# Reordering the opening of a fused linear-attention and SwiGLU kernel: last v pair on two engines, q tiles 1 and 3 moved, one k load merged

## The chip, the cores and the metric

The kernel runs on one core of one Trainium2 chip. The metric is device time in microseconds (us) of one execution; lower is better. "Median" is over the executions of one kernel in one measurement. Every profiled execution that is compared here had a granted TensorE clock of 0.99 or more. "Span" is the length of the profiled execution inside its trace; it is shorter than the device time of the same execution (before: 324.5 and 326.26).

## The reference

Eight batches of eight heads, 576 tokens and 64 columns go through a linear attention with cosine weights. Its output, 4608 rows of 512, goes through a root-mean-square norm and a gated feed-forward part.

```python
def phi(x, c, s):
    r = np.maximum(x, 0.0)
    return np.concatenate([r * c, r * s], axis=-1)
q_p = phi(q, cos_w, sin_w)
k_p = phi(k, cos_w, sin_w)
kv = np.einsum('bhsf,bhsd->bhfd', k_p, v)
z = np.sum(k_p, axis=2)
num = np.einsum('bhsf,bhfd->bhsd', q_p, kv)
den = np.einsum('bhsf,bhf->bhs', q_p, z)[..., None] + 1e-06
x = num / den                                   # then (4608, 512)
xn = x / np.sqrt(np.mean(x * x, -1) + 1e-06) * rms_g
g = xn @ w_gate                                 # 512 -> 1536
out = (g * sigmoid(g) * (xn @ w_val)) @ w_out   # 1536 -> 512
```

## The kernel before

In the timelines each engine's instructions come in the order of the calls (TensorE's from 17.26 to 21.15 us of the kernel before are the calls of the second block below, one after the other), so the code is read here as the order on each engine. A call names its engine (A is ScalarE, V is VectorE, G is GpSimd) or is TensorE's (names with pe, mm or nd; fillers keep TensorE busy with products that nothing reads). The names in the traces: `qp` is weighted q, `qpT` its transpose, `kvzs` the copy of k times v with z, `xt` a tile of x, `scr` its squares, `rs` the inverse root, `xn` the normalised x, `xnT` its transpose, `hT` the hidden activations, `vvm` and `vvt` the large and the small part of v in bf16, and `rk`, `rv`, `rq` what the loads bring.

The opening, from the last pieces of v to the first normalised tile (cut):

```python
    kvz_mm(0, low_banks, LOW)
    kvz_copy(A, 0, 0, low_banks[0], LOW)
    kvz_copy(A, 0, 1, low_banks[1], LOW)
    v_cast(V, 0, 3, 4, 0, 5)               # the last v pair, both on VectorE
    v_cast(V, 0, 3, 4, 5, NJ)
    kvz_mm(0, high_banks, (2, 3))
    nd_half(0, 0, 0, psV[0])               # first numerators, half a tile
    nd_post_half(0, 0, 0, psV[0])
    x_gain(0, 0, 0)                        # x times the gain, ahead of the inverse root
    q_tr_evac(A, 0, 1, psO[0][:, :], (0, 4))
    kvz_mm(0, high_banks, (3, 4))
    ...
    filler(7, psV[1][:, :])
    q_tr_pe(0, 2, psO[0][:, :])
    x_scale(0, 0)                          # then times the inverse root
```

The feed-forward part starts while q tiles 2 and 3 of batch 0 are still to be transposed:

```python
    q_phi(A, 0, 3, 1)
    q_tr_evac(A, 0, 2, psO[0][:, :])
    x_norm(0, 1)
    q_phi(V, 0, 3, 0)
    open_ffn(0, (0, 1), 0, 128)            # steps 0 and 1, first 128 tokens
    x_tr_pe(0, 1, psV[1][:, :])
    x_tr_evac(V, 0, 1, psV[1][:, :])
    q_tr_pe(0, 3, psO[1][:, :])            # transposes of q tile 3 ...
    nd_pe(0, 2, psA)
    nd_post(0, 2, psA)
    q_tr_evac(A, 0, 3, psO[1][:, :])       # ... their copy ...
    x_sq(0, 2)
    wo_load(0)
    open_ffn(0, (0, 1), 128, 256)
    open_ffn(1, (2,), 0, 256, parts=(0,))
    nd_pe(0, 3, psA)                       # ... and the user of that copy
    nd_post(0, 3, psA)
```

The loads that matter later are all on SyncE's queue and are taken in order:

```python
    load_kv("k", 1, 0, 1)                  # one row of k of batch 1, in the prologue
    ...
    d = load_kv("k", 1, 1, 4)              # the other three rows, after most weights
    tc.add_manual_dep(d.ins, weight_dmas[5].ins.name, SYNC_DEP, reason="after most weights")
    gate_q = load_q(1)                     # q of batch 1, behind the gate weights
    ...
    w = wo_load(1)                         # output weights, behind q of batch 1
    tc.add_manual_dep(w.ins, gate_q.ins.name, SYNC_DEP, reason="after q of batch 1")
    ...
    at(0, 10, "post", q_phi, V, 1, 0, 0)   # weighted q of batch 1, behind step 10
    ...
    if (which, nb) == ("v", 3):            # pieces of v of batch 3, behind steps 13 and 14
        at(b, 13, "post", load_heads, "v", nb, 0, 4)
        at(b, 14, "post", load_heads, "v", nb, 4, 8)
        at(b, 14, "post", load_last, "v", nb)
```

Of the kernel before, what the change touches and what calls it, by code (L numbers as in the profile page):

```python
# [9 lines left out]
FP32 = mybir.dt.float32  # L10
BF16 = mybir.dt.bfloat16
AF = mybir.ActivationFunctionType
ALU = mybir.AluOpType
# [13 lines left out]
def kernel(  # L27
# [11 lines left out]
    nc = tc.nc  # L39
    B, H, S, D = q.shape  # L40
    DM = H * D
# [32 lines left out]
    def load_kv(which, b, r0=0, r1=4, j0=0, j1=NJ):  # L74

        key = (which, b)
        if key not in raw:
            raw[key] = (two if which == "k" else one).tile(
                [P, 4, NJ * D], FP32, name=f"r{which}", tag=f"r{which}"
            )  # L80
        src = {"k": k, "v": v}[which]
        return nc.sync.dma_start(
            out=raw[key][:, r0:r1, j0 * D : j1 * D],
            in_=src[b, 2 * r0 : 2 * r1, :, :]
            .rearrange("h s d -> (h s d)")
            .rearrange("(r p n) -> p r n", p=P, n=NJ * D)[:, :, j0 * D : j1 * D],
        )
# [80 lines left out]
    load_kv("v", 0, 3, 4, 0, 5)  # L168
    load_kv("v", 0, 3, 4, 5, NJ)
    load_q_tokens(4, NJ)  # L170
    load_kv("k", 1, 0, 1)
    nc.scalar.preload_act_table(AF.Silu)
    gb = one.tile([P, DM], FP32, name="gb")

# [106 lines left out]
            src = flat[:, 2048:2304].rearrange("p (i d) -> p i d", d=D)  # L281
        phi(eng, kp_of(b)[:, 8 * c : min(8 * c + 8, 36), o], src, f(c))

    def q_phi(eng, b, c, part):
        o = slice(0, D) if part == 0 else slice(D, F)
        f = cos_of if part == 0 else sin_of
        if (b, c) not in qp_tiles:
            qp_tiles[(b, c)] = four.tile(
                [P, H if c < 4 else 4, F], BF16, name="qp", tag="qp" if c < 4 else "qpt"
            )  # L290
        if b == 0:
            for i in range(2 if c < 4 else 1):
                j = 2 * c + i
                f = cos_of if part == 0 else sin_of
                phi(
                    eng, qp_tiles[(b, c)][:, 4 * i : 4 * i + 4, o],
                    raw[("q", 0)][:, :, j * D : (j + 1) * D], f(5 + j),
                )
            return
        src = view4(raw[("q", b)], c) if c < 4 else raw[("qt", b)][:, :, :]  # L300
        phi(eng, qp_tiles[(b, c)][:, :, o], src, f(c))
# [15 lines left out]
    def q_tr_pe(b, c, bank):  # L317
        t = qp_tiles[(b, c)]
        dst = bank.bitcast(BF16).rearrange("p (h s) -> p h s", s=P)
        for h in range(H if c < 4 else 4):  # L320
            nc.tensor.transpose(dst[:, h, :], t[:, h, :], ident[:, :])  # L321

    def q_tr_evac(eng, b, c, bank, heads=(0, 8)):
        h0, h1 = heads if c < 4 else (0, 4)
        if b == 0:
            src = bank.bitcast(BF16).rearrange("p (i h s) -> p h i s", i=2, h=H)
            copy(
                eng, q_dst(b, c)[:, h0:h1, :].rearrange("p h (i s) -> p h i s", i=2),
                src[:, h0:h1, :, :],
            )  # L330
            return
        dst = bank.bitcast(BF16).rearrange("p (h s) -> p h s", s=P)
        copy(eng, q_dst(b, c)[:, h0:h1, :], dst[:, h0:h1, :])
# [7 lines left out]
    def v_cast(eng, b, r0=0, r1=4, j0=0, j1=NJ):  # L341
        copy(
            eng, vvm[b % 2][:, r0:r1, j0:j1, 0:D],
            raw[("v", b)][:, r0:r1, j0 * D : j1 * D].rearrange("p r (j d) -> p r j d", d=D),
        )
# [34 lines left out]
    def kvz_mm(b, banks, rs=(0, 4)):  # L380

        for r in range(*rs):
            for j in range(NJ):
                for c in range(2):
                    lo = 64 * c
                    nc.tensor.matmul(  # L386
                        banks[c][:, r * E : (r + 1) * E],
                        lhsT=kp_main[b][lo : lo + 64, j, r, :],
                        rhs=vvm[b % 2][lo : lo + 64, r, j, :],
                        start=(j == 0), stop=(j == NJ - 1),  # L390
                    )
# [4 lines left out]
    def kvz_copy(eng, b, c, bank, rs=(0, 4)):  # L396
        if (b, c) not in kvzs:
            kvzs[(b, c)] = three.tile([P, 4 * E], BF16, name="kvzs", tag=f"kvzs{c}")
        lo, hi = rs[0] * E, rs[1] * E
        copy(eng, kvzs[(b, c)][:, lo:hi], bank[:, lo:hi])  # L400
# [75 lines left out]
    def x_sq(b, j):  # L476
        xt = x_of[(b, j)]
        scr = one.tile([P, DM + 1], BF16, name="scr", tag="scr")
        ms = four.tile([P, 1], FP32, name="ms", tag="ms")
        nc.scalar.activation(  # L480
            out=scr[:, :], in_=xt[:, 0 : DM + 1], func=AF.Square,
            scale=1.0 / math.sqrt(DM), accum_out=ms[:, :],
        )
        rs = four.tile([P, 1], FP32, name="rs", tag="rs")
        nc.gpsimd.tensor_tensor(out=rs[:, :], in0=ms[:, :], in1=mhalf[:, :], op=ALU.pow)  # L485
        rs_of[(b, j)] = rs

    xn_of = {}
    xg = three.tile([P, DM], FP32, name="sg", tag="sg")

    def x_gain(b, j, g):

        c = slice(g * DM // 2, (g + 1) * DM // 2)
        nc.vector.tensor_tensor(
            out=xg[:, c], in0=x_of[(b, j)][:, c], in1=gb[:, c], op=ALU.mult
        )

    def x_scale(b, j):
        xn = four.tile([P, DM], BF16, name="xn", tag="xn")
        nc.vector.tensor_scalar(  # L500
            out=xn[:, :], in0=xg[:, :], scalar1=rs_of[(b, j)][:, :], scalar2=None, op0=ALU.mult
        )
        xn_of[(b, j)] = xn

    def x_norm(b, j):
        xn = four.tile([P, DM], BF16, name="xn", tag="xn")
        nc.vector.scalar_tensor_tensor(  # L507
            out=xn[:, :], in0=x_of[(b, j)][:, 0:DM], scalar=rs_of[(b, j)][:, :], in1=gb[:, :],
            op0=ALU.mult, op1=ALU.mult,
        )  # L510
        xn_of[(b, j)] = xn
# [22 lines left out]
    def x_tr_evac(eng, b, j, bank, part=(0, 4)):  # L534
        dst = bank.bitcast(BF16).rearrange("p (t s) -> p t s", s=P)
        copy(eng, x_dst(b, j)[:, part[0] : part[1], :], dst[:, part[0] : part[1], :])
# [54 lines left out]
    def filler(n, bank):  # L591
        for _ in range(n):
            nc.tensor.matmul(bank, lhsT=warm[:, 0:P], rhs=warm[:, :], start=True, stop=True)  # L593
# [25 lines left out]
    def gval_slice(c0, c1):  # L619
        weight_dmas.append(weight_slice(wg, moe_w_gate, c0, c1))  # L620
        weight_dmas.append(weight_slice(wv, moe_w_val, c0, c1))
# [29 lines left out]
    low_banks = [psG[1][:, :], psV[1][:, :]]  # L651
    high_banks = [psA[:, c, :] for c in range(2)]
    kvz_mm(0, low_banks, LOW)
    kvz_copy(A, 0, 0, low_banks[0], LOW)
    kvz_copy(A, 0, 1, low_banks[1], LOW)
    v_cast(V, 0, 3, 4, 0, 5)
    v_cast(V, 0, 3, 4, 5, NJ)
    kvz_mm(0, high_banks, (2, 3))
    nd_half(0, 0, 0, psV[0])
    nd_post_half(0, 0, 0, psV[0])  # L660
    x_gain(0, 0, 0)
    q_tr_evac(A, 0, 1, psO[0][:, :], (0, 4))
    kvz_mm(0, high_banks, (3, 4))
    kvz_copy(A, 0, 0, high_banks[0], HIGH)
    kvz_copy(A, 0, 1, high_banks[1], HIGH)
    filler(1, idle)
    nd_half(0, 0, 1, psO[1])
    nd_post_half(0, 0, 1, psO[1])
    q_tr_evac(A, 0, 1, psO[0][:, :], (4, 8))
    q_phi(A, 0, 2, 1)  # L670
    x_sq(0, 0)
    nd_pe(0, 1, psA)
    nd_post(0, 1, psA)
    x_gain(0, 0, 1)
    q_phi(A, 0, 2, 0)
    x_sq(0, 1)
    gval_slice(768, 1152)
    gval_slice(1152, 1536)
    filler(7, psV[1][:, :])
    q_tr_pe(0, 2, psO[0][:, :])  # L680
    x_scale(0, 0)

    def open_ffn(pair, steps, c0, c1, first=0, parts=(0, 1)):

# [26 lines left out]
    for half, (eng, bank) in enumerate(((A, psG[1]), (V, psV[1]))):  # L711
        part = (2 * half, 2 * half + 2)
        x_tr_pe(0, 0, bank[:, :], part)
        x_tr_evac(eng, 0, 0, bank[:, :], part)
    q_phi(A, 0, 3, 1)
    q_tr_evac(A, 0, 2, psO[0][:, :])
    x_norm(0, 1)
    q_phi(V, 0, 3, 0)
    open_ffn(0, (0, 1), 0, 128)
    x_tr_pe(0, 1, psV[1][:, :])  # L720
    x_tr_evac(V, 0, 1, psV[1][:, :])
    q_tr_pe(0, 3, psO[1][:, :])
    nd_pe(0, 2, psA)
    nd_post(0, 2, psA)
    q_tr_evac(A, 0, 3, psO[1][:, :])
    x_sq(0, 2)
    wo_load(0)
    open_ffn(0, (0, 1), 128, 256)
    open_ffn(1, (2,), 0, 256, parts=(0,))
    nd_pe(0, 3, psA)  # L730
    nd_post(0, 3, psA)
    open_ffn(1, (3,), 0, 256, first=1, parts=(0,))
    x_norm(0, 2)
    open_ffn(1, (2, 3), 0, 256, parts=(1,))
    open_h(0, 0, 0)
# [34 lines left out]
    def at(blk, n, where, f, *args):  # L770
        slots.setdefault((blk, n), none())[where].append((f, args))
# [2 lines left out]
        for f, args in slots.get((blk, n), none())[where]:  # L774
            f(*args)

    d = load_kv("k", 1, 1, 4)
    tc.add_manual_dep(d.ins, weight_dmas[5].ins.name, SYNC_DEP, reason="after most weights")
    gate_q = load_q(1)
    tc.add_manual_dep(  # L780
# [10 lines left out]
    for j in range(NJ):  # L791
        at(0, 7 + max(0, j - 1) // 2, "post", k_phi, V, 1, j, 0)
        at(0, 7 + max(0, j - 1) // 2, "post", k_phi, A, 1, j, 1)
    at(0, 10, "post", q_phi, V, 1, 0, 0)
    at(0, 11, "post", q_phi, A, 1, 0, 1)


# [216 lines left out]
```

## Time and profile before

| | before |
|---|---|
| median of 3, then of 6 runs | 326.24 us, 326.26 us |
| span of the profiled execution | 324.5 us |
| TensorE busy | 316.2 us, 97% |
| first matmul of the feed-forward part | 17.26 us |
| first 512-column matmul, which ends the opening | 29.98 us |
| first transpose of q of batch 1 | 41.20 us |
| first product of k and v of batch 3 | 97.47 us |
| end of the last copy of an output tile | 321.19 us |

The last rows are marks on TensorE's timelines. Between two marks TensorE does the same products in every kernel of this study (the fillers lie ahead of the first mark), so a difference in the distance between two marks is waiting time. That is the tool of this document: effects of some tenths of a microsecond are lost in the time of a whole run but stand out in such a distance. TensorE's timeline of the kernel before, with start, length, engine, line, operation, output and inputs, shapes, count:

```profile
29.98 1.03 PE L546 MATMUL psG<-xnT,wg 128*128 128x512 bf16 x3
...
41.20 0.61 PE L321 MATMUL psV<-ident,qp 128*128 128x128 bf16 x8
...
97.47 0.29 PE L370 MATMUL psA<-vvm,kpm 128*128 128x65 bf16 x4
97.59 0.19 PE L370 MATMUL psA<-vvt,kpm 128*128 128x65 bf16 x1
```

There is no bracket with an idle time at any of the four: TensorE waits for nothing there. The last two lines show that the product on the small part of v follows 0.12 us behind that on the large part.

### The profile page before, as it was taken

How to read it: one execution, taken by the hardware profiler on the slowest of the kernel's cores; microseconds unless marked ns; L12 is line 12 of the kernel's file. 1: busy time of each engine (PE TensorE's matmuls, PEld its weight loads, DVE VectorE, ACT ScalarE, POOL GpSimd, SP SyncE). 2: the span in 40 equal slices, each digit the busy share in tenths (PEclk: the TensorE clock that was granted, in tenths of full speed). 3: DMA queues.
4: the chain of work that ended last, by engine and by line, in shares of the span. 5: the costliest groups of instructions: out<-in, count | busy, mean ns of one | idle time of the engine just before them, and what ended most of it. 6: DMA issues, size and time to landing. Idle time of an engine off the chain costs nothing.

```text
span 324.5 us, 6131 instructions
## 1 busy us (share of the span) xinstructions
PE 316.2 (97%) x2249; PEld 162.4 (50%) x2284; DVE 184.3 (57%) x398; ACT 173.8 (54%) x351; POOL 39.3 (12%) x85
## 2 busy tenths in 40 slices
PE   8999999999999999999999999999999999999995
PEld 3588465555445444554454445444544444444443
DVE  6875768787656765578267745772577133203410
ACT  6974865965665556645555466455644333223321
POOL 4660202001111110012001120120011000000000
PEclk9999999999999999999999999999999999999999
DMA  7999999898799775977597679856611400020014
GB/s 271 281 196 253 309 205 339 243 165 189 164 248 273 190 205 153 237 163 195 165 214 206 155 219 210 194 158 215 128 40 33 131 32 0 25 106 0 1 33 100
DMA packets 89377, 53.90 MB, mean 166 GB/s; under 512 B 56321, under 2 KB 81921, under 8 KB 89346
## 3 DMA queue, kind: packets, MB, share of 16 engines
q1 hardware_dynamic: 82304, 48.65, 57.4%
q0 software_dynamic: 6880, 4.72, 10.0%
q8 instruction: 18, 0.29, 0.4%
q10 hardware_dynamic: 162, 0.13, 0.2%
q14 instruction: 13, 0.11, 0.1%
HBM read 37.75 MB, written 9.44 MB: 145 GB/s over the span
## 4 chain that ended last, share of the span: by engine, by line
PE 93%; DVE 2%; ACT 2%; issue 1%; POOL 0%; DVEq 0%
PE psC L566 26%; PE psV L546 26%; PE psG L546 26%; PE psA L414 2%; PE psO L593 2%; PE psA L370 2%; PE psG L566 2%; PE psO L692 1%; PE psG L692 1%; PE psV L692 1%; PE psV L321 1%; ACT kpm L252 1%; PE psA L386 1%; ACT sg L555 0%; PE psA L422 0%
## 5 line engine op out<-in xcount | busy, mean ns | idle before, releaser
L561 DVE TENSOR_TENSOR hT<-psV,sg 128x512 bf16<-128x512 f32 x102 | 70.3, 689 | 96.0 <-PE psV L546 71.2
L555 ACT ACTIVATE sg<-psG 128x512 f32<-128x512 f32 x102 | 60.6, 594 | 64.5 <-PE psG L546 63.2
L546 PE MATMUL psV<-xnT,wv 128*128 128x512 bf16 (+1 forms) x365 | 92.1, 375 | 0.4
L546 PE MATMUL psG<-xnT,wg 128*128 128x512 bf16 (+1 forms) x352 | 90.9, 375 | 0.7
L566 PE MATMUL psC<-wo,hT 128*128 128x512 bf16 x382 | 88.2, 380 | 0.7
L546 PEld LDWEIGHTS <-wv 128*128 128x128 bf16 x416 | 40.6, 98 | 47.4
L566 PEld LDWEIGHTS <-hT 128*128 128x128 bf16 x420 | 40.2, 98 | 46.7
L546 PEld LDWEIGHTS <-wg 128*128 128x128 bf16 x416 | 38.5, 98 | 40.8 <-DVE xnT L339 0.4
L485 POOL TENSOR_TENSOR rs<-ms,mhalf 128x1 f32<-128x1 f32 x36 | 19.8, 549 | 187.6 <-ACT scr L480 187.6
L337 ACT COPY osb<-psC 128x512 f32<-128x512 f32 (+1 forms) x33 | 19.1, 579 | 43.1 <-PE psC L566 42.4
L507 DVE SCALAR_TENSOR_TENSOR xn<-xt,rs,gb 128x512 bf16<-128x512 f32 x35 | 26.5, 757 | 16.4 <-POOL rs L485 16.3
L480 ACT ACTIVATE scr<-xt 128x513 bf16<-128x513 f32 x36 | 22.9, 635 | 23.7 <-DVE xt L469 23.6
L252 ACT ACTIVATE kpm<-rk,tab 128x256 bf16<-128x256 f32 (+2 forms) x58 | 28.2, 545 | 1.5 <-DMA rk<-in_k_dram 1.5
L469 DVE TENSOR_TENSOR xt<-psA,rec 128x512 f32<-128x512 f32 x35 | 24.2, 691 | 1.2
L252 ACT ACTIVATE qp<-rq,tab 128x512 bf16<-128x512 f32 (+1 forms) x37 | 23.7, 661 | 0.0
L254 DVE TENSOR_SCALAR kpm<-rk,tab 128x128 bf16<-128x128 f32 (+2 forms) x64 | 20.5, 377 | 2.1 <-DMA rk<-in_k_dram 2.1
L254 DVE TENSOR_SCALAR qp<-rq,tab 128x512 bf16<-128x512 f32 (+1 forms) x37 | 16.0, 452 | 0.0
L414 PEld LDWEIGHTS <-qpT 128*128 128x128 bf16 x248 | 11.7, 98 | 6.7 <-issue 0.3
L414 PE MATMUL psA<-kvzs,qpT 128*128 128x65 bf16 x248 | 12.8, 194 | 0.3
L546 PE MATMUL psG<-xnt_tail,wg 128*128 128x512 bf16 x48 | 12.3, 379 | 0.1
L546 PE MATMUL psV<-xnt_tail,wv 128*128 128x512 bf16 x47 | 12.1, 379 | 0.0
L339 DVE CAST vvm<-rv 128x1024 bf16<-128x1024 f32 (+4 forms) x16 | 10.4, 674 | 0.0
(99 smaller groups left out, 183.8 us busy)
## 6 DMA issues: line engine op xcount, KB each, us to landing
out_dram<-osb SPq DMA_DIRECT2D x28, 256.0 KB, 2.5
rk<-in_k_dram SPq DMA_DIRECT2D x20, 256.0 KB, 3.2
rq<-in_q_dram SPq DMA_DIRECT2D x20, 256.0 KB, 3.1
rv<-in_v_dram SPq DMA_DIRECT2D x16, 256.0 KB, 3.2
rq<-in_q_dram SPq DMA_DIRECT2D x2, 1024.0 KB, 9.2
out_dram<-osb SPq DMA_DIRECT2D x14, 128.0 KB, 3.2
rv<-in_v_dram SPq DMA_DIRECT2D x3, 576.0 KB, 8.4
wo<-in_moe_w_out_dram POOLq DMA_DIRECT2D x4, 384.0 KB, 7.1
```

What stands on the lines that cost most here:

```text
L252: nc.scalar.activation(out=out_ap, in_=in_ap, func=AF.Relu, scale=scale)
L254: eng.tensor_scalar(out=out_ap, in0=in_ap, scalar1=scale, scalar2=0.0, op0=ALU.mult, op1=ALU.max)
L337: nc.scalar.copy(out=o, in_=i)
L414: nc.tensor.matmul(o[:, g, i, :], lhsT=qpT[(b, 0)][:, h, j * P : (j + 1) * P], rhs=kvz_of(b, h), start=True, stop=True,)
L469: nc.vector.tensor_tensor(out=xt[:, 0:DM].rearrange("p (b h d) -> p b h d", b=2, d=D), in0=o[:, :, :, 0:D], in1=rec[:, :, :].unsqueeze(3). ...
L480: nc.scalar.activation(out=scr[:, :], in_=xt[:, 0 : DM + 1], func=AF.Square, scale=1.0 / math.sqrt(DM), accum_out=ms[:, :],)
L485: nc.gpsimd.tensor_tensor(out=rs[:, :], in0=ms[:, :], in1=mhalf[:, :], op=ALU.pow)
L507: nc.vector.scalar_tensor_tensor(out=xn[:, :], in0=x_of[(b, j)][:, 0:DM], scalar=rs_of[(b, j)][:, :], in1=gb[:, :], op0=ALU.mult, op1=ALU. ...
L546: nc.tensor.matmul(pst[bank][:, cols[0] : cols[1]], lhsT=w[:, t, n * P : (n + 1) * P], rhs=x[:, t, cols[0] : cols[1]], start=(t == 0), sto ...
L555: nc.scalar.activation(out=sg[:, :], in_=psG[bank][:, :], func=AF.Silu)
L561: nc.vector.tensor_tensor(out=hTs[blk][:, n, :], in0=psV[bank][:, :], in1=sg[:, :], op=ALU.mult)
L566: nc.tensor.matmul(bank, lhsT=hTs[blk][:, n, j * P : (j + 1) * P], rhs=wo[:, n, :], start=(n == 0), stop=(n == NNT - 1),)
```

## The change

The intent is an earlier first x tile and fewer waits of TensorE in the opening. **Part 1**: the last v pair is cast by ScalarE and VectorE side by side, and all its products come ahead of the first numerators; the copies of q tile 1 stand behind them. **Part 2**: the gain and the inverse root are applied to x tile 0 in one combined multiply, as to all other tiles. **Part 3**: q tile 3 is transposed later, behind the work of two x tiles. **Part 4**: the first weighted q of batch 1 moves from behind step 10 to behind step 11 on VectorE. **Part 5**: the early load of one row of k of batch 1 is gone; the later load brings all four rows.

```diff
-    load_kv("k", 1, 0, 1)
...
+    v_cast(A, 0, 3, 4, 0, 5)
+    v_cast(V, 0, 3, 4, 5, NJ)
+    kvz_mm(0, high_banks, HIGH)
     kvz_copy(A, 0, 0, low_banks[0], LOW)
     kvz_copy(A, 0, 1, low_banks[1], LOW)
-    v_cast(V, 0, 3, 4, 0, 5)
-    v_cast(V, 0, 3, 4, 5, NJ)
-    kvz_mm(0, high_banks, (2, 3))
     nd_half(0, 0, 0, psV[0])
     nd_post_half(0, 0, 0, psV[0])
-    x_gain(0, 0, 0)
-    q_tr_evac(A, 0, 1, psO[0][:, :], (0, 4))
-    kvz_mm(0, high_banks, (3, 4))
...
+    x_norm(0, 0)
...
-    filler(7, psV[1][:, :])
-    q_tr_pe(0, 2, psO[0][:, :])
-    x_scale(0, 0)
+    filler(9, psV[1][:, :])
...
+    q_tr_pe(0, 2, psO[0][:, :])
+    q_tr_evac(A, 0, 2, psO[0][:, :])
     q_phi(A, 0, 3, 1)
-    q_tr_evac(A, 0, 2, psO[0][:, :])
     x_norm(0, 1)
-    q_phi(V, 0, 3, 0)
+    q_phi(V, 0, 3, 0, (0,))
     open_ffn(0, (0, 1), 0, 128)
     x_tr_pe(0, 1, psV[1][:, :])
     x_tr_evac(V, 0, 1, psV[1][:, :])
-    q_tr_pe(0, 3, psO[1][:, :])
+    q_phi(V, 0, 3, 0, (1,))
     nd_pe(0, 2, psA)
     nd_post(0, 2, psA)
+    open_ffn(0, (0, 1), 128, 256)
+    q_tr_pe(0, 3, psO[1][:, :])
     q_tr_evac(A, 0, 3, psO[1][:, :])
     x_sq(0, 2)
     wo_load(0)
-    open_ffn(0, (0, 1), 128, 256)
     open_ffn(1, (2,), 0, 256, parts=(0,))
+    open_ffn(1, (3,), 0, 256, first=1, parts=(0,))
     nd_pe(0, 3, psA)
     nd_post(0, 3, psA)
-    open_ffn(1, (3,), 0, 256, first=1, parts=(0,))
...
-    d = load_kv("k", 1, 1, 4)
+    d = load_kv("k", 1)
...
-    at(0, 10, "post", q_phi, V, 1, 0, 0)
+    at(0, 11, "post", q_phi, V, 1, 0, 0)
```

More of the change, by code (lines that the diff above doesn't have):

```diff
@@ L282, in k_phi_as_q, with q_phi @@
         phi(eng, kp_of(b)[:, 8 * c : min(8 * c + 8, 36), o], src, f(c))
-    def q_phi(eng, b, c, part):
+    def q_phi(eng, b, c, part, subs=(0, 1)):
         o = slice(0, D) if part == 0 else slice(D, F)
@@ L291, in q_phi @@
         if b == 0:
-            for i in range(2 if c < 4 else 1):
+            for i in subs if c < 4 else (0,):
                 j = 2 * c + i
@@ L488 @@
     xn_of = {}
-    xg = three.tile([P, DM], FP32, name="sg", tag="sg")
-    def x_gain(b, j, g):
-        c = slice(g * DM // 2, (g + 1) * DM // 2)
-        nc.vector.tensor_tensor(
-            out=xg[:, c], in0=x_of[(b, j)][:, c], in1=gb[:, c], op=ALU.mult
-        )
-    def x_scale(b, j):
-        xn = four.tile([P, DM], BF16, name="xn", tag="xn")
-        nc.vector.tensor_scalar(
-            out=xn[:, :], in0=xg[:, :], scalar1=rs_of[(b, j)][:, :], scalar2=None, op0=ALU.mult
-        )
-        xn_of[(b, j)] = xn
     def x_norm(b, j):
@@ L653 @@
     kvz_mm(0, low_banks, LOW)
+    v_cast(A, 0, 3, 4, 0, 5)
+    v_cast(V, 0, 3, 4, 5, NJ)
+    kvz_mm(0, high_banks, HIGH)
     kvz_copy(A, 0, 0, low_banks[0], LOW)
     kvz_copy(A, 0, 1, low_banks[1], LOW)
-    v_cast(V, 0, 3, 4, 0, 5)
-    v_cast(V, 0, 3, 4, 5, NJ)
-    kvz_mm(0, high_banks, (2, 3))
     nd_half(0, 0, 0, psV[0])
     nd_post_half(0, 0, 0, psV[0])
-    x_gain(0, 0, 0)
-    q_tr_evac(A, 0, 1, psO[0][:, :], (0, 4))
-    kvz_mm(0, high_banks, (3, 4))
     kvz_copy(A, 0, 0, high_banks[0], HIGH)
     kvz_copy(A, 0, 1, high_banks[1], HIGH)
-    filler(1, idle)
     nd_half(0, 0, 1, psO[1])
     nd_post_half(0, 0, 1, psO[1])
-    q_tr_evac(A, 0, 1, psO[0][:, :], (4, 8))
-    q_phi(A, 0, 2, 1)
+    q_tr_evac(A, 0, 1, psO[0][:, :])
     x_sq(0, 0)
@@ L673 @@
     nd_post(0, 1, psA)
-    x_gain(0, 0, 1)
-    q_phi(A, 0, 2, 0)
+    q_phi(A, 0, 2, 1, (0,))
+    q_phi(V, 0, 2, 0, (0,))
+    x_norm(0, 0)
+    q_phi(V, 0, 2, 0, (1,))
     x_sq(0, 1)
+    q_phi(A, 0, 2, 1, (1,))
     gval_slice(768, 1152)
     gval_slice(1152, 1536)
-    filler(7, psV[1][:, :])
-    q_tr_pe(0, 2, psO[0][:, :])
-    x_scale(0, 0)
+    filler(9, psV[1][:, :])
     def open_ffn(pair, steps, c0, c1, first=0, parts=(0, 1)):
```

## The prediction

> **What bounds the kernel now.** I read the busy table first, then the chain of waits, then the timelines of each engine from 8 to 31 us and from 39 to 46 us, where the diff acts.
>
> ```profile
> PE 316.2 (97%) x2249; PEld 162.4 (50%) x2284; DVE 184.3 (57%) x398; ACT 173.8 (54%) x351; POOL 39.3 (12%) x85
> ...
> PE 93%; DVE 2%; ACT 2%; issue 1%; POOL 0%; DVEq 0%
> ```
>
> TensorE is busy 97% and holds 93% of the chain that ends last. The diff removes no product that the result needs, so it can only move idle gaps of TensorE. Nearly all of those that it touches lie in the opening, where the chain leaves TensorE:
>
> ```profile
> 14.56 0.72 ACT scr L480 x2
> 15.28 0.29 ACT qp L252
> ...
> 16.77 0.56 POOL rs L485
> 17.33 0.02 issue
> 17.36 0.75 DVE xn L507
> 18.11 0.82 DVE qp L254 x2
> 18.93 0.14 issue
> 19.07 0.38 PE psO L321 x4
> 19.45 0.25 PE psA L414 x8
> ```
>
> Columns are start, length, engine, tile. Squares of x tiles (scr), their inverse root (rs) and normalised tiles (xn) decide when TensorE has work; before 17.26 us it runs fillers (seven, 13.87 to 15.55 us). From 17.26 us it works on the feed-forward part. There it stands still twice more, for about 0.12 us before the first half of the transposes of q tile 3 and 0.31 us before the second (they wait for the qp at 18.11): 0.43 us in all. From 19.07 to 30 us I find no gap worth naming. So the opening has little left to win: at most those 0.43 us plus what an earlier first x tile gives.
>
> **What the Trainium skill says.** (1) Perfetto Trace Analysis, Optimization Strategy: find the gaps on the engine in question within one regime and ask what unblocks them; and its section on the most-contended engine warns that matmul busy time says little of headroom. The trace agrees: 97% busy includes fillers, so I count gaps, not percent. (2) VectorE: DVE Perf Modes, the perf-mode tier table: a tensor_scalar on fp32 in SBUF runs 2x, a tensor_tensor 1x, and a PSUM operand lowers the tier. The trace agrees in kind: scaling the first x tile by one scalar took 0.49 us, the combined multiply that replaces it takes 0.75 us. (3) ScalarE: Activation LUTs, Rules for kernel authors: about 0.3 us per ACTIVATE plus 0.83 ns per element. The trace has 0.676 us for a cast of 576 columns and 1.14 us for 1152, so 0.81 ns each and 0.21 us fixed. (4) DMA: Bandwidth & Descriptors, Queues, rings and completion order: each DMA engine goes round-robin between queues by packets. The trace agrees: from 26 to 30 us both queues move data, about 0.22 MB per us on the SyncE queue and 0.08 on the software queue.
>
> **Part 1, the last v pair and its products.** Now VectorE casts both pieces, 0.68 us from 11.31 us. After, ScalarE casts 320 columns: estimated from the two casts above as 0.21 + 320 x 0.81 ns = 0.47 us, in 11.22 to 11.69. ScalarE has 0.27 us idle there, so the copies of the low kv are about as late as now (11.60 instead of 11.58). The 36 high products, now in two parts ending at 12.72, run in one go and end near 12.2. First numerators start 12.08 instead of 11.90 and VectorE begins on them 0.14 later, at 12.50. It then does two half tiles of 0.83 us without the 0.42 us gain multiply between them: x tile 0 is whole at 14.07 instead of 14.46, 0.39 earlier.
>
> **Part 2, the first x tile's chain.** Square and accumulator read 0.73 us after a 0.10 wait (14.17 to 14.90), inverse root 0.57 (14.98 to 15.55; the weight issues leave GpSimd free from 14.72), then the combined multiply of 0.75 instead of 0.49: done 16.32 against 16.46. Of 0.39 us, 0.26 is paid back for the dearer multiply. Transposes and two evacuations follow as now (0.75 from transpose to first matmul): 17.10 instead of 17.26. The transposes of q tile 2 (8, 0.45 us) now fit into that evacuation wait, so they cost nothing; nor did they before, beside fillers. Two more fillers lie in idle time. **Gain 0.16 us.**
>
> **Part 3, the moved transposes of q tile 3.** Order on TensorE is now: steps 0 and 1 for 128 columns (0.90, to 18.00), transposes of x tile 1 (end of result 18.40), numerators of tile 2 (0.22), then steps 0 and 1 for the next 128 columns, which need VectorE's copy of x tile 1 (0.41 us, 18.42 to 18.83). With only the numerators in between, TensorE idles from about 18.5 to 18.87: 0.38 us. That takes the place of the 0.43 us gone. Then 0.90 us, the q transposes 0.45, their result at 20.38. The lines of now:
>
> ```profile
> 19.49 1.01 ACT L337 COPY qpT<-psO 128x1024 bf16<-128x1024 bf16 x1 [0.58 <-PE psO L321]
> ...
> 20.91 0.40 PE L414 MATMUL psA<-kvzs,qpT 128*128 128x65 bf16 x8
> ...
> 21.80 0.69 DVE L469 TENSOR_TENSOR xt<-psA,rec 128x512 f32<-128x512 f32 x1
> ...
> 22.40 0.74 DVE L507 SCALAR_TENSOR_TENSOR xn<-xt,rs,gb 128x512 bf16<-128x512 f32 x1
> ...
> 23.34 0.39 PE L532 MATMUL psA<-ident,xn 128*128 128x128 bf16 x4
> ```
>
> The copy of q tile 3 is done at 20.50 and numerators 3 come 0.41 us later: no wait. After the change the copy runs 20.42 to 21.42, and only two steps (0.87 us) lie between the transposes and numerators 3: TensorE is ready at 21.09 and idles to 21.46, **0.37 us**. The delay carries on: VectorE makes x tile 3 (it ends 1.58 us after those numerators began, 23.04) before it normalises x tile 2 (0.75, to 23.69), so the transposes of x tile 2 wait to 23.72, another **0.28 us**, and those of x tile 3 lose about 0.06. The squares of x tile 2 queue behind the 1.0 us copy, but their root is there by 22.70 and doesn't bind.
>
> Sum: -0.16 - 0.43 + 0.38 + 0.37 + 0.28 + 0.06 = 0.50; following the clock instead, the step after x tile 3 begins at 25.98 where it began at 25.55: **+0.43 us**, which I take. After it TensorE has no gap up to 30 us to win it back.
>
> **Part 4, the q work of batch 1, moved by a step.**
>
> ```profile
> 40.28 0.47 DVE L254 TENSOR_SCALAR qp<-rq,tab 128x512 bf16<-128x512 f32 x1
> 40.67 0.68 DVE L561 TENSOR_TENSOR hT<-psV,sg 128x512 bf16<-128x512 f32 x1
> ```
>
> TensorE begins the transposes that need this qp at 41.20. Behind the hT product, which cannot start before the step's last matmul ends near 40.51, the qp runs 41.13 to 41.60. TensorE waits from 41.20 to about 41.63: **+0.43 us**, with all times before shifted alike. Nothing fills it, since engines run in program order.
>
> **Part 5, the loads.** One row of k for batch 1 (288 KB) leaves the early queue and joins the later load of that k. The early one overlaps the first weights for only half a microsecond (12.0 to 12.5), so weights land some 0.3 us earlier; those were in time already. The later load grows from 864 to 1152 KB. It waits as now for the sixth weight slice (SyncE waited 16.6 us for it); estimated at the 0.22 MB per us above, its 1.18 MB take 5.4 us from about 25.6 and land near 32, while ScalarE first uses them at 33.26 plus the shift. q of batch 1 slips by about 0.5 us, to 39.2, ahead of use after 40.2. No wait; **0 us**.
>
> **Sum.** 0.43 + 0.43 = +0.86 us: 326.24 + 0.86 = 327.10.
>
> **The rivals.** (a) The author's aim holds: the opening ends 0.2 to 0.4 us sooner, because TensorE never waits for the q copy or the x copy. For it: x tile 0 is ready 0.39 us earlier and the idle 0.12 and 0.31 disappear. Against it: the 1.01 us copy with 0.87 us of work before its user. It would give about 325.9. I give it 25%. (b) A load becomes the bound: the larger k load or the q behind it comes late, ScalarE stands before its k work, its Silu behind that, and TensorE waits. For it: the DMA engines are 90% busy throughout the opening, and the q work was moved back as if q came later. Against it: estimated margins of 1.4 us and more. It would add 0.5 to 1.5 us: about 328. I give it 15%. (c) My four waits come as worked out: 60%. (d) The late qp is hidden because TensorE waits there anyway: the trace shows none between 40.5 and 44 us, and it would take 0.43 off (c), inside the range.
>
> **Range and chances.** The weighted effect is 0.60 x 0.86 - 0.25 x 0.3 + 0.15 x 1.5 = +0.67, so 326.9. The range takes in (a) at its lower end and the milder cases of (b) at the upper: 325.9 to 327.6. Two per cent is 6.5 us; the whole opening holds under 2 us of TensorE gaps, so faster and slower by that much are near 1% each, slower a little likelier through loads.
>
> **What would show it.** In the timeline after: first matmul of the feed-forward part near 17.1; a gap near 18.5 to 18.9 before steps 0 and 1 of the second 128 columns; numerators 3 right behind a q copy ending near 21.4; transposes of x tile 2 near 23.7; the end of the opening (now 29.98, the first 512-column matmul) at 30.4; transposes of q of batch 1 right behind a VectorE qp, 0.86 us later than now, at 42.06. If the first 512-column matmul starts before 30.0, part 3 is wrong; if those q transposes come straight behind the output products, part 4 is; if ScalarE waits for a DMA at its k work of batch 1, part 5 is.

## The result and the profile after

The kernel got slower: a median of **328.30 us** (328.04 to 328.83, 6 runs) against 326.26 us (326.21 to 326.45, 6 runs). The ratio is 1.0064, with a 95% interval of 1.0051 to 1.0077. Here and below, a ratio is the mean time of one kernel's fast runs over that of the other's of the same rounds, so it is not quite the ratio of the medians. The prediction was 326.9 with a range up to 327.6, so the direction was right, but the loss of 2.04 us is outside the range and far above the 0.86 us of its own sum.

The page of the kernel after, busy time by engine and the chain by engine:

```profile
PE 318.2 (97%) x2285; PEld 162.1 (50%) x2285; DVE 184.2 (56%) x397; ACT 173.5 (53%) x349; POOL 39.7 (12%) x85
...
PE 87%; ACT 4%; DVE 3%; DMA 3%; SPq 1%; issue 1%; POOL 0%; ACTq 0%; DVEq 0%
```

TensorE's share of the chain fell from 93% to 87%, and DMA and SyncE's issue (SPq), which the chain before did not have, now hold 4%. Of this, 3.69 us is only the first load of k at the start, where the chain before ran over fillers; 7.79 us is a load of v at 91 to 99 us. So somewhere in the middle the end depends on a load. This is the first sign of what the prediction lacked. The opening in the chain of waits of the kernel after:

```profile
14.30 0.73 ACT scr L479 x2
...
15.11 0.67 POOL rs L484
...
15.80 0.76 DVE xn L490
...
18.67 0.43 DVE xnT L338
...
20.68 1.02 ACT qpT L336
...
21.75 0.43 PE psA L413 x8
...
22.64 0.69 DVE xt L468
...
24.05 0.40 PE psA L515 x4
```

The squares of x tile 0 begin 0.26 us earlier than before (14.30 against 14.56). Further down, the chain leaves TensorE at the three places that were foreseen: for the copy of x tile 1 (18.67), for the copy of q tile 3 (20.68, 1.02 long, with its user right behind it at 21.75) and for x tile 3 and what queues behind it (22.64), up to the transposes of x tile 2 at 24.05, which stood at 23.34 before.

The marks, in TensorE's timeline of the kernel after:

```profile
30.78 0.59 PE L529 MATMUL psG<-xnT,wg 128*128 128x512 bf16 x2
...
42.64 0.61 PE L320 MATMUL psV<-ident,qp 128*128 128x128 bf16 x8 [0.48 <-DVE qp L253]
...
98.91 0.28 PE L369 MATMUL psA<-vvm,kpm 128*128 128x65 bf16 x4
99.50 0.19 PE L369 MATMUL psA<-vvt,kpm 128*128 128x65 bf16 x1 [0.31 <-POOL vvt L338]
```

A bracket gives TensorE's idle time and what ended it. Two of the four marks have one now: the transposes of q of batch 1 wait for VectorE, and the first product on the small part of v of batch 3 waits for GpSimd's cast of it, 0.59 us behind the product before it where it was 0.12. The chain of waits says what the cast had waited for:

```profile
90.81 3.30 SPq L121
94.16 4.49 DMA rv<-in_v_dram
...
98.71 0.75 POOL vvt L338
```

That cast also took longer than before, and VectorE works on a cast of its own at that time. The kernel after, VectorE and GpSimd:

```profile
98.50 0.70 DVE L338 CAST vvm<-rv 128x1024 bf16<-128x1024 f32 x1
98.71 1.20 POOL L338 CAST vvt<-rv 64x256 bf16<-64x256 f32 x2 [6.87 <-DMA rv<-in_v_dram]
```

and before:

```profile
97.01 0.89 DVE L339 CAST vvm<-rv 128x1024 bf16<-128x1024 f32 x1
96.92 1.25 POOL L339 CAST vvt<-rv 64x256 bf16<-64x256 f32 x2 [6.52 <-DMA rv<-in_v_dram]
```

Before, GpSimd's first cast of the small v starts 0.09 us ahead of VectorE's cast of the large v, takes 0.43 us (to 97.35), and VectorE's takes 0.89. After, it starts 0.21 us behind VectorE's, takes 0.74 us (to 99.45) and ends 0.25 us after VectorE's has ended. So the later landing cost twice here: the cast started later and took longer.

The distances between the marks, worked out by subtraction from both traces, divide the whole difference (us):

| stretch | before | after | change | predicted |
|---|---|---|---|---|
| start to the first feed-forward matmul | 17.26 | 17.35 | +0.09 | -0.16 |
| from there to the first 512-column matmul | 12.72 | 13.43 | +0.71 | +0.59 |
| from there to q of batch 1 | 11.22 | 11.86 | +0.64 | +0.43 |
| from there to the first product of batch 3 | 56.27 | 56.27 | 0.00 | 0 |
| from there to the product on the small v | 0.12 | 0.59 | +0.47 | 0 |
| from there to the end of the last copy | 223.60 | 223.58 | -0.02 | 0 |
| from the last copy to the end of the span | 3.30 | 3.69 | +0.39 | 0 |
| span | 324.5 | 326.8 | +2.3 | +0.86 |

Two rows are what was predicted, somewhat larger. Two rows, 99 us and the tail, are nowhere in the prediction: 0.86 us together.

### The profile page after: what moved, and what is told of

It is laid out like the page before. It is cut to its first block, busy times and chain, and to the rows that moved or that the text cites. A ratio compares the mean times of both kernels' runs of the same rounds, so it can differ in the third digit from the quotient of the medians.

```text
span 326.8 us, 6161 instructions
## 1 busy us (share of the span) xinstructions
PE 318.2 (97%) x2285; PEld 162.1 (50%) x2285; DVE 184.2 (56%) x397; ACT 173.5 (53%) x349; POOL 39.7 (12%) x85
## 4 chain that ended last, share of the span: by engine, by line
PE 87%; ACT 4%; DVE 3%; DMA 3%; SPq 1%; issue 1%; POOL 0%; ACTq 0%; DVEq 0%
PE psC L549 25%; PE psG L529 25%; PE psV L529 25%; PE psA L413 2%; ACT kpm L251 2%; PE psA L369 2%; DMA rv<-in_v_dram 1%; PE psG L549 1%; DMA rk<-in_k_dram 1%; SPq L121 1%; PE psG L671 1%; PE psA L385 1%; PE psV L671 1%; PE psO L671 1%; PE psV L320 1%
## 5 line engine op out<-in xcount | busy, mean ns | idle before, releaser
L529 PE MATMUL psG<-xnT,wg 128*128 128x512 bf16 (+1 forms) x368 | 92.8, 374 | 0.1
L549 PE MATMUL psC<-wo,hT 128*128 128x512 bf16 x396 | 89.4, 379 | 0.0
L251 ACT ACTIVATE qp<-rq,tab 128x512 bf16<-128x512 f32 (+1 forms) x35 | 22.8, 669 | 0.0
L253 DVE TENSOR_SCALAR qp<-rq,tab 128x512 bf16<-128x512 f32 (+1 forms) x39 | 16.7, 448 | 0.0
L338 DVE CAST vvm<-rv 128x1024 bf16<-128x1024 f32 (+3 forms) x15 | 10.0, 687 | 0.0
```

The source lines that it names most:

```text
L251: nc.scalar.activation(out=out_ap, in_=in_ap, func=AF.Relu, scale=scale)
L253: eng.tensor_scalar(out=out_ap, in0=in_ap, scalar1=scale, scalar2=0.0, op0=ALU.mult, op1=ALU.max)
L529: nc.tensor.matmul(pst[bank][:, cols[0] : cols[1]], lhsT=w[:, t, n * P : (n + 1) * P], rhs=x[:, t, cols[0] : cols[1]], start=(t == 0), sto ...
L549: nc.tensor.matmul(bank, lhsT=hTs[blk][:, n, j * P : (j + 1) * P], rhs=wo[:, n, :], start=(n == 0), stop=(n == NNT - 1),)
```

## The experiments

The theory: the order of q tile 3 costs 0.7 us in the opening, the moved step of q costs 0.64 us, and the merged load of k costs the rest, as it makes a later load late. The rivals: the waits are chance of one profiled execution; the wait at 99 us comes from the delay as such and not from the load; the tail has nothing to do with the load. Twelve runs in three groups, each group with its own runs of the kernel before (medians 326.40, 326.41 and 326.44 us). In the first group the runs of before were noisy, 326.14 to 328.25 us, so its ratios are too. All kernels gave correct results.

**1. The changed kernel again** (after_again), no edit.

> The changed kernel once more, as the yardstick of this group. Theory: three separate waits of TensorE, which come again in every run: the opening ends 0.8 us later than before (first 512-column matmul at 30.8 us against 29.98), the transposes of q of batch 1 wait 0.6 us for a VectorE qp, and at 99 us the products of batch 3 wait 0.4 us for the last v load. Time 328.0 to 328.8 us, 1.9 to 2.3 us over the kernel before. Rival: the wait at 99 us is chance (a DMA issue on SyncE took 3.3 us in that one execution) and is not there this time; then the last product ends about 1.45 us later than before instead of 1.89.

Median 328.11 us, ratio 1.0043 (1.0024 to 1.0062). Every distance came back: 13.43, 11.86, a wait at the small v of 0.54 - 0.12 = 0.42 us, a tail of 3.68. So these are properties of the kernel and not chance of one execution. One thing did not come back: SyncE's issue ahead of the late v took 3.30 us in the first trace and 0.42 us in this one, where the transfer took 7.27 us instead of 4.49. The slow issue itself is chance; the late landing came in both traces.

**2. The step of q undone in the changed kernel** (undo_q_step).

```diff
-    at(0, 11, "post", q_phi, V, 1, 0, 0)
+    at(0, 10, "post", q_phi, V, 1, 0, 0)
```

> The changed kernel with one edit undone: VectorE's qp of batch 1 back behind step 10. Theory (VectorE's program order makes the wait): the transposes of q start 0.8 us later than before instead of 1.44, and the time falls by 0.64 us against the changed kernel of the same group. Rival (with the whole k load put late, q of batch 1 lands too late for step 10, and VectorE would stand before it): no gain or a loss, and the trace shows VectorE waiting for the q load near 41 us.

Median 327.61 us, ratio 1.0039 (1.0012 to 1.0066). The distance to q of batch 1 is 11.22 again, as before the change, and the wait at the small v is gone (0.12); the tail stays at 3.72. The median is 0.50 us below that of after_again, where 0.64 was expected; the span of the profiled execution is 1.1 us shorter (325.6 against 326.7), and one of the six runs took 329.68.

**3. The step of q alone, in the kernel before** (only_q_step): the reverse edit.

> The kernel before with one edit of the change alone: VectorE's qp of batch 1 behind step 11 instead of step 10. Theory: the transposes of q wait for it whatever the opening does; +0.43 to +0.64 us, 326.7 to 326.9. Rival (the move only costs together with late loads): within 0.1 us of before, 326.2 to 326.4.

Median 327.14 us, ratio 1.0015 (0.9994 to 1.0037). The time alone would be inconclusive. The trace is not: all stretches are those of before but one, 11.86 instead of 11.22. **The step costs 0.64 us**, by itself and in company. VectorE's timeline of the kernel after shows what of it the prediction missed:

```profile
41.41 0.69 DVE L544 TENSOR_TENSOR hT<-psV,sg 128x512 bf16<-128x512 f32 x1 [0.45 <-PE psV L529]
42.02 1.67 DVE L253 TENSOR_SCALAR qp<-rq,tab 128x512 bf16<-128x512 f32 x4
```

Set against the first 512-column matmul (30.78), the qp starts 11.24 us in, where the prediction had 41.13 - 29.98 = 11.15: 0.09 more. The first of its four takes 0.47 us as before the change, so it ends near 42.49, and TensorE starts its transposes at 42.64, 0.15 us after that and not 0.03: 0.12 more.

**4. The order of q tile 3 undone in the changed kernel** (undo_q3_order): the block of part 3 goes back to the order of before.

```diff
     q_tr_pe(0, 2, psO[0][:, :])
-    q_tr_evac(A, 0, 2, psO[0][:, :])
     q_phi(A, 0, 3, 1)
+    q_tr_evac(A, 0, 2, psO[0][:, :])
...
-    q_phi(V, 0, 3, 0, (0,))
+    q_phi(V, 0, 3, 0)
...
-    q_phi(V, 0, 3, 0, (1,))
+    q_tr_pe(0, 3, psO[1][:, :])
...
-    open_ffn(0, (0, 1), 128, 256)
-    q_tr_pe(0, 3, psO[1][:, :])
...
+    open_ffn(0, (0, 1), 128, 256)
     open_ffn(1, (2,), 0, 256, parts=(0,))
-    open_ffn(1, (3,), 0, 256, first=1, parts=(0,))
     nd_pe(0, 3, psA)
     nd_post(0, 3, psA)
+    open_ffn(1, (3,), 0, 256, first=1, parts=(0,))
```

> The changed kernel with the order of the block around q tile 3 as before (transposes of q tile 3 right behind those of x tile 1, numerators 3 after one step). Theory (the order of this block makes the opening longer): the waits before numerators 3 and before the transposes of x tile 2 go, the opening ends within 0.2 us of before (first 512-column matmul 29.9 to 30.2), and the time falls by 0.6 to 0.8 us. Rival (the loss sits in the parts before 17.4 us, the v casts and the dearer multiply): the opening still ends at 30.5 or later and the time falls by less than 0.3 us.

Median 327.70 us, ratio 1.0030 (1.0009 to 1.0051). The stretch fell from 13.43 to 12.53, below the 12.72 of the kernel before. The wait at the small v is gone here too (0.12). The median is 0.41 us below that of after_again, short of the 0.6 to 0.8 that were expected. The profiled execution had a late start, 17.62 us, with 7.89 us of its chain in a load of v of batch 0; whether the other runs had it isn't known.

**5. The order of q tile 3 alone, in the kernel before** (only_q3_order): the reverse edit, and nothing else of the change.

> The kernel before with part 3 of the change alone (order around q tile 3, with its two halves of VectorE's qp). Theory (this order makes the stretch from the first feed-forward matmul to the first 512-column matmul longer: 13.43 us in two runs of the changed kernel, 12.72 before, 12.52 with part 3 undone): 13.3 to 13.5 us here, and the time rises by 0.6 to 0.8 us. Rival (the longer stretch needs the earlier first tile of parts 1 and 2, or the loads): 13.0 us or less, time up by less than 0.3 us.

Median 327.18 us, ratio 1.0018 (1.0004 to 1.0032). TensorE's timeline of this kernel:

```profile
19.19 0.38 PE L692 MATMUL psG<-xnT,wg 128*128 128x128 bf16 x4 [0.27 <-DVE xnT L339]
...
30.82 1.03 PE L546 MATMUL psG<-xnT,wg 128*128 128x512 bf16 x4
```

With its first feed-forward matmul at 17.37, the stretch is 30.82 - 17.37 = 13.45 us, and the first of the lines has the wait for the copy of x tile 1. **The order costs 13.45 - 12.72 = 0.73 us** with the old first tile; with the new one it is 13.43 - 12.53 = 0.90.

**6. The new first tile alone** (first_tile_only): the changed kernel with parts 3, 4 and 5 undone, by the three edits shown.

> Parts 1 and 2 of the change alone: the changed kernel with the order around q tile 3, the k load and VectorE's qp of batch 1 all as before. Theory (parts 1 and 2 win nothing and lose next to nothing: the first x tile is whole 0.2 us sooner, but the dearer multiply and a slower inverse root give it back): feed-forward begins at 17.2 to 17.4 us against 17.26, the opening ends 29.95 to 30.2 against 29.98, no wait at 41 or 99 us; time 0 to 0.4 us over before, the upper end if the last 0.4 us behind the last copy, seen in every variant of the changed kernel so far, shows here too. Rival (parts 1 and 2 carry the loss of the opening): opening ends after 30.4.

Median 326.21 us, ratio 0.9996 (0.9982 to 1.0010): no difference in time that the interval would show. In the trace the first feed-forward matmul stands at 17.27, where it stood before (17.26), but the stretch behind it is 12.53 instead of 12.72. The gain of parts 1 and 2 is thus 0.19 us, and not where it was predicted: the qp of q tile 3 is whole sooner, so all eight of its transposes run from 18.62 us and the next step starts at 19.34 us, 2.07 us into the stretch instead of 19.53 - 17.26 = 2.27.

**7. The merged load of k alone, in the kernel before** (only_k_load).

```diff
-    load_kv("k", 1, 0, 1)
...
-    d = load_kv("k", 1, 1, 4)
+    d = load_kv("k", 1)
```

> The kernel before with the k load of batch 1 in one piece behind the weights. Theory: the load has room, no engine waits for it (ScalarE's first use at 33.3 us is 1 us or more behind its landing), q of batch 1 slips by about 1 us but is in time for step 10; within 0.15 us of before. Rival (the load is what made the changed kernel move the qp a step later): VectorE waits for q before 41 us and the time rises by 0.3 us or more.

Median 327.01 us, ratio 1.0019 (1.0006 to 1.0031): **the part that was predicted at zero costs about 0.6 us**. In the trace two stretches differ from before, apart from a start that was 0.19 us later: from q of batch 1 to batch 3 it is 56.43 instead of 56.27, and the tail is 3.69 instead of 3.30. For the first, VectorE's and GpSimd's timelines of this kernel:

```profile
40.47 0.48 DVE L253 TENSOR_SCALAR qp<-rq,tab 128x512 bf16<-128x512 f32 x1 [0.18 <-DMA rq<-in_q_dram]
```

```profile
40.99 2.44 POOL L632 DMA_DIRECT2D wo<-in_moe_w_out_dram  x3 [16.82 <-DMA rq<-in_q_dram]
```

and the same row of GpSimd in the kernel before:

```profile
38.68 2.34 POOL L633 DMA_DIRECT2D wo<-in_moe_w_out_dram  x3 [14.70 <-DMA rq<-in_q_dram]
```

GpSimd's loads of output weights wait for q of batch 1, so their start tells when q has landed: 2.31 us later than before, where the prediction had estimated 0.5. That is enough for VectorE to wait for q itself, though not for TensorE, whose distance to q of batch 1 stays at 11.22. The output weights, behind q on purpose, are issued as much later; TensorE's first product with them behind the third q transposes starts 0.58 us after those (45.40 to 45.98) in place of 0.46 (45.18 to 45.64). That this is a wait for these weights is possible, but the trace names no releaser. Nor is it shown that these 0.16 us belong to the load: in the other six traces with k in one piece GpSimd's loads start between 39.60 and 40.12 us, and there the stretch stays at 56.27 or 56.28 us.

**8. The same number of loads with the merged k** (k_load_and_split): experiment 7, and a later load split in two, so that SyncE issues as many loads as before.

```diff
-            load_kv("k", 2)
+            load_kv("k", 2, 0, 1)
+            load_kv("k", 2, 1, 4)
```

> The kernel before with the k load in one piece, as in only_k_load, and the k load of batch 2 split in two, so that SyncE issues as many loads as in the kernel before. Theory (the 0.4 us behind the last copy depends on the number of instructions ahead of the end, not on when k lands): the end takes 2.75 to 2.8 us again, time 0.4 us below only_k_load, 326.6. Rival (it comes from the later loads themselves): 3.1 us or more again, 327.0.

Median 326.41 us, ratio 0.9995 (0.9981 to 1.0009): the time of before. The tail is 3.31 us again, though k of batch 1 comes as in experiment 7. So **the 0.39 us at the end hang on the number of SyncE's load instructions, and not on when k lands.** One thing that differs in the tail can be seen in the view of DMA queues in a narrow window. Of the kernel before, 323.1 to 323.5 us:

```profile
q14 instruction: 1, 0.01, 9.2%
```

and of the kernel after, 326.3 to 326.8 us:

```profile
q14 instruction: 1, 0.01, 6.4%
```

In both, one packet of an instruction queue is the last transfer of the program. It starts at 323.31 us before and at 326.42 us after. Set against the landing of the last output, worked out from the packets of all fourteen traces:

| | last output landed | instruction packet | end of span |
|---|---|---|---|
| before | 323.07 | 0.24 later | 1.41 after the landing |
| k_load_and_split | 323.05 | 0.07 later | 1.43 after |
| the other six with the old number of SyncE loads | | 0.2 to 0.5 later | 1.40 to 1.42 after |
| after | 324.97 | 1.45 later | 1.80 after |
| only_k_load | 323.44 | 1.45 later | 1.80 after |
| the other four with one load fewer | | 1.46 to 1.47 later | 1.80 to 1.83 after |

In the six kernels with one load fewer, the end follows the start of the packet by 0.34 to 0.37 us; in the eight others by 0.91 to 1.35. It would be easy to say that the end waits for this packet, but it does not: the time is lost earlier. The packed trace also has SyncE's closing instructions, which wait for the outputs and which the views of `prof` leave out. In the kernel after, SyncE's 335th recorded instruction ends at 325.43 us, when all outputs have landed, but its 336th starts only at 325.79. Behind it the instructions follow with the spacing of the kernel before to within 0.02 us, and one more of them than before (0.07 us) has to come after the landing. The packet starts 0.63 us after the 336th.

All fourteen traces fit one place. In the six with one load fewer, 0.36 to 0.38 us pass ahead of SyncE's 336th recorded instruction, and the last output has landed by then. In k_load_and_split, with two instructions more, 0.36 us pass ahead of the 336th too (322.10 to 322.47), but there the last output lands only at 323.05, so nothing is lost. In the seven others, with one more, the 336th is the very instruction that waits for the last output, which would hide the gap. So the gap sits at a fixed place in SyncE's program, and one load instruction fewer moves it from ahead of the last landing to behind it. The Trainium skill (Runtime: NRT & Kernel Launch, Instruction fetch mechanics) says that each engine fetches its instructions in blocks of 256 over a DMA queue of its own and that the cost of crossing a block is mostly hidden. That this gap is such a crossing is an inference and was not tried by itself; if it is, it is not hidden in these six kernels.

**9. The old loads of k in the changed kernel** (undo_k_load): the reverse of the edit of experiment 7.

> The changed kernel with the k load of batch 1 split as before. Theory: the 0.4 us behind the last copy, which all six kernels with the single k load have (3.13 to 3.23 us from the end of the last issue to the end of the span) and none of the four others (2.75 to 2.79), goes; q of batch 1 lands about 1.5 us sooner; the waits in the opening and before the q transposes stay; the wait for v of batch 3 at 99 us stays, since it comes from the lateness of that v load against the products; 0.4 us or a little more below the changed kernel. Rival: the wait for v at 99 us also comes from the k load, by way of the order of loads on the queue, and goes with it: 0.8 us.

Median 327.57 us, ratio 1.0033 (1.0018 to 1.0047). The tail is 3.29. At batch 3, TensorE's timeline:

```profile
99.25 0.29 PE L370 MATMUL psA<-vvm,kpm 128*128 128x65 bf16 x4
99.38 0.19 PE L370 MATMUL psA<-vvt,kpm 128*128 128x65 bf16 x1
```

No wait: the small part follows in 0.13 us, although this execution came there at 99.25, later than the kernel after did (98.91). So in the traces the wait at 99 us is not of the delay as such; it goes with the merged load, which was the rival here: the theory was that it would stay. But it does not come with the merged load alone either: experiments 2, 4 and 7 have the load without the wait. It came in the two traces that have the load and both late stretches. How firm this is, the two casts show. In all twelve traces without the wait GpSimd's first cast of the small v starts ahead of VectorE's last cast of the large v and takes 0.39 to 0.57 us; in the two with the wait it starts 0.21 and 0.13 us behind it and takes 0.74 and 0.81. In this run it was ahead by only 0.07 us. So a slightly later landing could have brought the wait here as well, and one trace is little to say that the merged load is needed for it.

**10. The small v of batch 3 loaded sooner, in the changed kernel** (last_v_sooner).

```diff
     at(b, 13, "post", load_heads, "v", nb, 0, 4)
+    at(b, 13, "post", load_last, "v", nb)
     at(b, 14, "post", load_heads, "v", nb, 4, 8)
-    at(b, 14, "post", load_last, "v", nb)
```

> The changed kernel with one further edit: the two small last pieces of v of batch 3 are asked for one step earlier, ahead of the second half of its heads. Theory (TensorE waits at 99 us for exactly these pieces and GpSimd's casts of them): the wait of 0.4 us at 99 us goes, the last product ends about 1.4 us later than before instead of 1.8, time 0.4 us below the changed kernel (328.1 to 328.3). Rival (the loads are late as a whole, so VectorE's casts of the heads are late in place of them): the wait stays at 0.3 us or more, under another name.

The wait is gone, so it was for this load: GpSimd casts at 97.04 us instead of 98.71. The time did not follow: 328.23 us, ratio 1.0058 (1.0046 to 1.0071). The profiled execution shows one reason, in TensorE's timeline:

```profile
18.07 0.40 PE L671 MATMUL psV<-xnT,wv 128*128 128x128 bf16 x4 [0.36 <-DMA wv<-in_moe_w_val_dram]
```

Here the second group of matmuls of the feed-forward part waited for the first value weights, and the stretch was 13.96 instead of 13.43 us: 0.53 lost where 0.47 was won. The edit acts 70 us later and can't have caused that. Whether all its timed runs had it can't be told from one trace. As they stand, 328.05 to 328.63 us, they show no gain over the changed kernel (328.04 to 328.83, and 327.88 to 328.50 in the first group), so what the wait at 99 us costs in time is **not shown by a run**; it is shown in the distances only.

**11. One half of a qp sooner, in the kernel before** (half_qp_sooner): VectorE's half of q tile 3 is itself split, and its first part is put ahead of the normalisation of x tile 1.

```diff
     x_scale(0, 0)
+    q_phi(V, 0, 3, 0, (0,))
...
-    q_phi(V, 0, 3, 0)
+    q_phi(V, 0, 3, 0, (1,))
```

> A try at beating both kernels: the kernel before, with the first half of VectorE's qp of q tile 3 put in front of its idle time at 16.46 us, by means of the argument that the change adds. Theory (in the kernel before TensorE waits 0.43 us for these two halves, behind the multiply of x tile 1): the transposes of q tile 3 start without a wait, the opening ends 0.3 to 0.4 us sooner (29.6 against 29.98), and the time falls as much, to about 325.9. Rival (the next wait takes its place at once, the copy of x tile 1 or of q tile 2): less than 0.15 us.

Median 326.03 us, ratio 0.9989 (0.9977 to 1.0002). The stretch is 12.42 instead of 12.72, so 0.30 of the 0.43 us of waits before q tile 3 can be had by moving the producer ahead instead of the user back. The interval of the time just reaches 1.

**12. Both gains together** (both_wins): experiment 6 with the edit of experiment 11, the first part of the qp behind `q_phi(A, 0, 2, 1, (1,))`.

> A try at beating both kernels: parts 1 and 2 of the change (first_tile_only, 0.2 us below before) with the first half of VectorE's qp of q tile 3 in VectorE's idle time ahead of the first x copy (half_qp_sooner, 0.38 us below before). Theory (they remove the same wait ahead of the transposes of q tile 3, so the gains overlap): feed-forward stretch 12.35 to 12.45 us beginning at 17.2 to 17.35, time 325.9 to 326.1. Rival (they add up): 12.2 us or less, time 325.8 or less.

Median **325.88 us** (325.77 to 326.17), ratio 0.9981 (0.9966 to 0.9997), faster than both kernels, 0.56 us below the 326.44 of its group. TensorE's timeline:

```profile
17.07 0.38 PE L673 MATMUL psG<-xnT,wg 128*128 128x128 bf16 x4
...
18.19 0.63 PE L321 MATMUL psO<-ident,qp 128*128 128x128 bf16 x8
...
29.48 1.03 PE L530 MATMUL psG<-xnT,wg 128*128 128x512 bf16 x4
```

The stretch is 12.41 us, that of experiment 11; the two gains do not add up in it, since both work on the same wait. The rest of the difference is the start, 17.07 us. Starts varied between 17.07 and 17.70 us over the fourteen traces, so how much of it belongs to this order is open. (The two latest, 17.62 and 17.70, are those of experiments 4 and 9, where the chain of the opening goes through a load of v of batch 0.)

## Why the prediction was wrong

Its direction was right, and its rival (a) (25%) fell. It was wrong in size, and in part 5 in mechanism too; step by step:

**Part 5, "No wait; 0 us", is the step that failed.** What it worked out for the load and for q held in the changed kernel, though with less room: k landed at 32.6 us (22.74 to 32.63 in the packed trace) where it has "near 32", ScalarE used it from 34.06, q landed at 39.3 where it has 39.2, and nothing waited for either. It failed in stopping there. It did not follow the queue to the loads with no slack, and it had no term for the length of SyncE's program. The first is 0.47 us in the changed kernel (0.42 when it ran again), the wait for the small v of batch 3, which goes with the load in the traces, though by a narrow margin (experiment 9); the second is the 0.39 us of the tail, SyncE's gap behind the last landing. Together they are 0.86 of the 1.42 us by which the change of the span exceeds the predicted sum. Measured alone, the load costs 327.01 - 326.41 = 0.60 us of time, of which the trace has 0.39 in the tail and 0.16 behind q of batch 1; the 0.16 is not in the changed kernel (56.27 us). Removing the merged load from the changed kernel leaves 327.57 us, 1.13 us above before; the changed kernel's own excess was 2.04 us, or 1.71 when it ran again.

**Part 3, +0.43 us to the end of the opening**: right in mechanism, with all three waits where they were foreseen. For the stretch its own numbers give +0.59 (30.41 - 17.10 = 13.31); it was +0.70 to +0.73. Counted from the first feed-forward matmul, numerators 3 came at 4.40 us (21.75 - 17.35) where the prediction has 4.36, the transposes of x tile 2 at 6.70 where it has 6.62, and the step after x tile 3 at 9.00 (26.35) where it has 8.88: each hand-over was some hundredths longer than counted.

**Part 4, +0.43 us**: right in mechanism, undersized. The terms are the start of the qp, 0.09 us later than worked out, and the hand-over from the qp to the transposes, taken as 0.03 us (41.60 to 41.63) and measured as 0.15: 0.43 + 0.09 + 0.12 = 0.64.

**Parts 1 and 2, -0.16 us at the first feed-forward matmul**: that gain was not seen there. The squares began at 14.30, sooner than before but 0.13 later than the predicted 14.17; the inverse root took 0.67 us in the chain instead of the 0.57 counted; the dearer multiply took its 0.26, as counted. The first two are 0.23 of the 0.25 us between 17.10 and 17.35. Part of the first of them is the start of this execution: the first copy of the low kv, which should have come 0.02 us later, came 0.11 later (11.69 against 11.58). The gain of 0.19 us came in the stretch instead, and only where part 3 was undone.

**The rival (b), a load becomes the bound**, had 15%, and its "about 328" is what was measured. A load did become a bound, but that the number fits is luck: the path that it names, ScalarE standing before its k work, did not come. The places were a v of batch 3 some 60 us later and the end of the program, and 1.35 of the 2.28 us of the table belong to parts 3 and 4.

One reading of the prediction shows less than it says: that both queues move data from 26 to 30 us does not show that a DMA engine takes turns between them. No number of its sum rests on that.

The parts measured one by one in the kernel before (time, except the last): parts 1 and 2 -0.20, part 3 +0.74, part 4 +0.74, part 5 +0.60, and the wait at 99 us +0.42 to +0.47 from traces. They sum to 2.30 to 2.35 us against a measured 2.04, each with an uncertainty of some tenths. Why the v of batch 3 lands later in the changed kernel, 60 us after the merged load, is **open**: in the kernel before GpSimd's cast came 0.09 us ahead of VectorE's, so little was needed.

## What to carry to other kernels

Before moving a copy's producer towards its user, count the work of the bounding engine that lies between them: 0.87 us of matmuls do not cover a copy of 1.01 us, and moving the producer ahead was worth more than moving the user back. Judge a moved or merged load by everything behind it on the same queue, down to the loads with no slack, and look at the end of the program as well. For changes under 1 us, compare distances between fixed marks in two traces, as the start of a program varies by as much as the effect.

## What the Trainium skill lacked or had wrong

- TensorE: Matmul & The Clock Gate, Back-to-back issue gap: it gives some 81 ns per matmul of 128 columns and 131 ns of 512 columns in a real stream of loads and matmuls. Here sixteen of 128 columns take 0.90 us (17.35 to 18.25 in the kernel after), so 56 ns each, and four of 512 columns in 0.86 us (92.00 to 92.86 us), so 216 ns each: the numbers that the page gives for an isolated gap.
- Runtime: NRT & Kernel Launch, Instruction fetch mechanics: it gives no time for crossing a block where it is not hidden. Here 0.36 to 0.38 us pass ahead of one instruction of SyncE, at the same place in all seven traces where it can be seen, and the end came 0.39 us later when one load instruction fewer moved that place behind the last landing. That it is such a crossing is inferred.
- I found on no page the spread of a first load's landing. ScalarE's and VectorE's first work on k began between 4.30 and 4.59 us in these kernels, and the first feed-forward matmul between 17.07 and 17.70.
